# Four start-up edits to a fused attention and MLP kernel: where a tile of x and a weight piece are sent from, how the map weights are folded, and the order that goes with it

## The chip, the cores and the metric

The kernel runs on one core of one Trainium2 chip. The metric is device time in microseconds (us) from launch to end. The time before is 149.91 us, the median of five runs (149.40 to 150.06).

The engines: TensorE multiplies matrices (PE in the profile; PEld is its weight load), VectorE (DVE) and ScalarE (ACT) work on elements and read PSUM, GpSimd (POOL) does elementwise work on SBUF, SyncE (SP) issues transfers. ScalarE issues some too.

## The reference, cut to what matters

One sequence of 2048 tokens, width D = 448, sixteen heads of 28, an MLP of width 1792, all in bfloat16. Two branches read the same layernorm and are added to the input:

```python
xn  = layernorm(x)
qkv = xn @ wqkv                                   # q, k, v: 16 heads of 28
pq, pk = q @ w_phi[h], k @ w_phi[h]               # a 28x28 map for each head
phi = lambda p: concat([softmax(p), softmax(-p)]) # 56 features a head
kv  = sum_s phi(pk)[s]^T v[s];  z = sum_s phi(pk)[s]
o   = (phi(pq) @ kv) / (phi(pq) @ z + 1e-6)       # linear attention
out = x + o @ wo + silu(xn @ w1) @ w2
```

Since the map has no non-linearity ahead of it, the kernel multiplies each head's columns of wqkv by its map once (the fold), and then uses the folded weights `Wqk` directly on xn. A softmax does not change when the same number is taken from all its inputs, so the fold also takes each head's last column from the other 27, and that last feature's exponential is the constant one.

## The kernel before, in words

Tokens are in 16 tiles of 128. The head of the program loads x tile by tile and the first pieces of w1, takes the layernorm of tiles 0 to 3 (`ln_tile`: statistics `bnst`, `bnag`, the root `ve` on ScalarE for tiles 0 to 3 and on GpSimd after, `rstd`, the normalised tile `xn`), transposes these four tiles on TensorE (`tr0a` to `tr3`) and starts three MLP blocks on them. Tiles 4 to 15 are transposed by DMA from SyncE (`xnT_dma5`, `xnT_dma7` and so on, two tiles each).

After that the work is in blocks: `F` is a pair of 128-column pieces of the first MLP product for 512 tokens (F0 to F6 for tiles 0 to 3, F7 to F13 for 4 to 7, and so on), `v`, `k`, `q` are the projections of two tiles. Each block fills two PSUM banks. It runs as two halves (`a` with three pairs, `b` with four pairs of matmuls): each matmul takes 64 rows, the lower and the upper row half of the array work beside each other and write different banks, and in the second half of a block they change banks. ScalarE then reads the two banks (silu for F, exponentials for k and q, a copy for v). `f` is the fold, `K` the sums over keys, `M` their masking, `s` the scaling of query features by GpSimd followed by a DMA transpose into `phT`, `U` attention of one tile, `Y` and `F n@bank` the second MLP product of a tile, `W` and `R` the output projection, `E` the last tile.

TensorE's order is written out by hand in `PLAN`, one word for each step with its banks behind the `@`; `strict` makes every TensorE instruction keep that order. The other engines' orders come from a list scheduler (`_Prog.schedule`) with assumed durations; within an engine the emitted order is then fixed, and each instruction waits on semaphores for what it depends on. `chain` adds order between instructions of one engine.

SyncE issues nearly all loads, in order: x tiles 0, 1, 2 and 3, pieces of w1, x tiles 4 to 7, the rest of w1, wv, x tiles 8 to 11, three weight transposes (`wT_dma0` to 2, straight from wqkv in DRAM), x tiles 12 to 15, `xnT_dma5`, `xnT_dma7`, five more weight transposes, the other `xnT` transposes, w2 and wo. ScalarE issues the head maps (`wphi`) and the second w1 piece (`w1_512`, columns 512 to 1023, first used by the third MLP block of the head).

The fold (`fold`, `fold_loads`, `fold_mms`, `fold_sub`): GpSimd spreads the maps into block-diagonal matrices of four heads (`BDphi`, 112 rows, with `maskh`); eight transposes bring wqkv's columns in groups of 112; each fold step does two of the four row tiles (`kt`) of D with sixteen full-array matmuls, 112 rows by 112 columns; ScalarE copies each head's last column, VectorE subtracts it, one subtraction for each row tile.

Of the kernel before, what the change touches and what calls it, by code (L numbers as in the profile page):

```python
# [6 lines left out]
BF16 = mybir.dt.bfloat16  # L7
F32 = mybir.dt.float32
# [132 lines left out]
class _Prog:  # L141
# [76 lines left out]
    def schedule(self):  # L218
# [55 lines left out]
        while done < n:  # L274
# [58 lines left out]
          ("pool", "pe"): 100.0}  # L333
PLAN = """aF3@4 bF3 aF6@0 aF4@2 bF4 bF6 av2@4 aF5@6 bv2 bF5 av0@2 aF12@0 aF13@4 bv0 bF12 bF13 aF11@6 bF11 f2@24 aF8@0 aF10@6 bF8
bF10 f0@24 aF9@0 aF7@6 bF9 bF7 ak2@4 bk2 av12@6 ak14@2 bv12 av10@0 bk14 bv10 ak4@4 av14@6 bk4 ak0@2 bv14 ak8@0 bk0 bk8
av6@6 Y2@5:1 Y2:9 Y2:4 ak6@2 av8@0 bv6 bv8 bk6 av4@6 ak10@4 bv4 bk10 ak12@2 aq4@0 bk12 K0-2 bq4 aq6@4 K2-4 bq6 aq8@2
K4-6 bq8 aq0@0 aF17@4 s4 K6-10 bq0 aF14@2 bF17 bF14 aF19@0 K10-12 bF19 aF16@4 K12-16 aF23@2 bF16 bF23 aF27@0 aF24@4 bF27
bF24 M aF20@2 aF25@0 bF20 aF15@4 bF25 aF26@2 aF22@6 bF26 aF18@0 s6 s8 bF22 bF15 bF18 aq2@6 aF21@2 aq10@4 bF21 bq2 aq12@0
bq10 bq12 F7@3:8 Y0@6:7 U9 Y1@5:6 F6@4:14 Y1:3 s0 F9@2:11 U6@1 Y1:5 U5 U7@0 Y0:7 F9:3 s2 Y3@1:10 Y3:4 W9 s10 s12 U10
U3@5 W6 F7:6 aq14@0 R9,6 bq14 U8 W7 F5@4:8 s14 F10@5:7 U0 F10:7 U11@6 U12@1 F5:6 U4@2 F4@0:10 W5 F8@7:12 W10 F4:4 F8:2  # L340
U2@1 W4 W0@6 W3@2 W8 R4,3 R8 R0,7,10,5 F13@1:14 F11@2:3 F12@6:4 F14@5:7 W2@3 U1@4 U13 F14:7 F11:2 F11:3 F12:1 F11:4 U14
F11:1 F11:1 W11 W1@4 F12:9 W12 U15 W13 W14 R14,12 R13,11 R1,2 F15@07:5 F15:5 F15:4 E15"""


def bass_parallel_sum__linear_kernel_hedgehog__dense_activation_silu__prompt_kernel(
# [12 lines left out]
    KP = 112  # L358
    G = 4
# [16 lines left out]
    with es:  # L376
        def sb(name, shape, dt):
            return es.enter_context(nc.sbuf_tensor(name, shape, dt))
# [12 lines left out]
        DQ = H * DF  # L391
        Wqk = sb("Wqk", [128, 2, 4, DQ], BF16)
        last27 = sb("last27", [128, 4, 2, H], F32)
        Wp = sb("Wp", [KP, G, DH], BF16)
        BDphi = sb("BDphi", [KP, G, KP], BF16)

# [23 lines left out]
        ones_bf = sb("ones_bf", [128, 128], BF16)  # L420
        ones4 = sb("ones4", [KP, 4], F32)
        mtmp = sb("mtmp", [KP, 4], F32)
        maskh = sb("maskh", [KP, 4], F32)
        mask2 = sb("mask2", [KP, 2], F32)
# [37 lines left out]
        def d_pool(n, per=1.0):  # L462
            return n * per + 120.0
# [24 lines left out]
        def act(dst, src, func, n, name, scale=1.0, table=None, **keys):  # L488
            P.op("act", d_act(n), lambda e: e.activation(dst, src, func, scale=scale),  # L489
                 reads=[src], writes=[dst], table=table, name=name, **keys)  # L490
# [8 lines left out]
        def load(dst, src, name, eng="sp", lat=1700.0):  # L499
            n = 2  # L500
            for _, cnt in list(dst.ap):
                n *= cnt
            P.dma(lambda e: e.dma_start(out=dst, in_=src), n / 280.0, writes=[dst], name=name, eng=eng, lat=lat)  # L503

        load(Wp[:], A_w_phi.rearrange("(g hl) d f -> (hl d) g f", g=G), "wphi", eng="act", lat=2500.0)
        memset(ones_bf[:], 1.0, 128, "ones")
# [5 lines left out]
        memset(ones4[:], 1.0, 4, "ones4")  # L512
        act(warm_act[:], ones_bf[:, 0:4], ACTF.Sqrt, 1750, "warm_act", table="sqrt")

        def block_mask(dst, w, n):
            tmp = mtmp[:, 0:n]
            P.op("pool", d_pool(4), lambda e: e.affine_select(tmp, ones4[:, 0:n], [[-w, n]], ALU.is_ge, 0.0,
                                                               base=0, channel_multiplier=1),
                 reads=[ones4[:]], writes=[tmp], name="mask1")
            P.op("pool", d_pool(4), lambda e: e.affine_select(dst, tmp, [[w, n]], ALU.is_ge, 0.0,  # L520
                                                               base=w - 1, channel_multiplier=-1),
                 reads=[tmp], writes=[dst], name="mask2")

        block_mask(maskh[:], DH, 4)

# [6 lines left out]

        def load_x(t0, t1):
            load(x_sb[:, t0:t1, :], xt[:, t0:t1, :], f"x{t0}", lat=1400.0)

# [7 lines left out]
        load_x(0, 1)  # L543
        load_x(1, 2)
        load_x(2, 4)
# [6 lines left out]
        load_x(8, 12)  # L552
        load_x(12, 16)
        load(w2_sb[:], B_w2.rearrange("(f p) d -> p f d", p=128), "w2")
        for i in range(2):
# [9 lines left out]

        bd4 = BDphi[:].rearrange("p g (h f) -> p g h f", h=4)

        def fold():
            P.op("pool", d_pool(448, 2.0), lambda e: e.tensor_tensor(
                bd4, Wp[:, :, None, :].broadcast_to([KP, G, 4, DH]),  # L570
                maskh[:, None, :, None].broadcast_to([KP, G, 4, DH]), ALU.mult),
                reads=[Wp[:], maskh[:]], writes=[BDphi[:]], name="bdphi")

        def fold_loads():
            for a in range(8):
                dma_t(wT_sb[:, a, :], A_wqkv[:, a * KP:a * KP + 128], 600.0, f"wT_dma{a}", 1800.0 if a == 2 else 1310.0, sbuf=False)

        def fold_mms(k0, slots):
            mms = []
            for kt, fb in zip((k0, k0 + 1), slots):  # L580
                for qk in range(2):
                    wps = banks[fb + qk][:, 0:G * KP].rearrange("p (g c) -> p g c", g=G)
                    mms += [(wps[:, g, :], wT_sb[0:KP, qk * 4 + g, KS[kt]:KS[kt] + 128], BDphi[:, g, :], True, True) for g in range(G)]
            P.cur_slack = 400.0
            pe_mms(mms, "fold", dur=50.0 * len(mms))
            P.cur_slack = 0.0
            for kt, fb in zip((k0, k0 + 1), slots):
                src = psum[:, fb * 512:(fb + 2) * 512].rearrange("p (b c) -> p b c", b=2)[:, :, 0:D].rearrange("p b (h f) -> p b h f", f=DH)
                ref = last27[:, kt, :, :]
                act(ref, src[:, :, :, DF], ACTF.Identity, 32, "fold_ref")  # L590
                dst = Wqk[:, :, kt, :].rearrange("p b (h f) -> p b h f", f=DF)
                fold_sub(dst, src[:, :, :, 0:DF], ref)

        def fold_sub(dst, src, ref):
            P.op("dve", d_dve(2 * DQ), lambda e: e.tensor_tensor(dst, src, ref[:, :, :, None].broadcast_to([128, 2, H, DF]), ALU.subtract),
                 reads=[src, ref], writes=[dst], name="fold_sub")
# [119 lines left out]
        def proj_block(t, b0, is_k):  # L716
            fns = pair_block(b0, DQ, lambda i, kt, r: xnT[r, t + i, kt, :],
                             lambda i, kt, r: Wqk[r, int(is_k), kt, :], "k" if is_k else "q")

            def evac():  # L720
                E2 = ek(t, 2)[:, :, 0:2 * D] if is_k else eq(t, 2)
                src = psum[:, b0 * 512:(b0 + 2) * 512].rearrange("p (i c) -> p i c", i=2)[:, :, 0:DQ].rearrange("p i (h f) -> p i h f", f=DF)
                dst = E2.rearrange("p i (h s f) -> p i h s f", s=2, f=DH)
                for sg in range(2):
                    act(dst[:, :, :, sg, 0:DF], src, ACTF.Exp, 2 * DQ, "exp", scale=(1.0 if sg == 0 else -1.0), table="exp", okeys_w=["acttab"])
                E4 = E2.rearrange("p i (h f) -> p i h f", f=DH)
                R2 = Rec[:, int(is_k), t:t + 2, :]
                step = 2 if is_k else 1
                for i in range(0, 2, step):
                    sums(E4[:, i:i + step], R2[:, i:i + step, :], step)  # L730
                if is_k:
                    scale_rows(t, is_k)

            return *fns, evac
# [158 lines left out]
        chain("bnst0 bnag0 bnst1 bnag1 rstd0 xn0a xn0 rstd1 xn1 bnst2 bnag2 bnst3 bnag3 rstd2 xn2 rstd3 xn3 ev3".split())  # L893
        chain("wphi warm_act w1_512 ve0 ve1 ev0a ev0 ev1 ve2 ve3 ev2 silu_table".split())
        fold_loads()
# [24 lines left out]
        chain("ev3 bnst4".split())  # L920
        block_mask(mask2[:], 2 * DH, 2)
        memset(vaug[:, :, :, DH], 1.0, 2150, "vaug1")
# [6 lines left out]
        for t in range(8, NT):  # L929
            ln_tile(t)  # L930
        chain("x8 wT_dma0 wT_dma1 wT_dma2 x12 xnT_dma5 xnT_dma7 wT_dma3 wT_dma4 wT_dma5 wT_dma6 wT_dma7 xnT_dma9 xnT_dma11 xnT_dma13 xnT_dma15 w2 "
              "wo0 wor0 wo1 wor1".split())
# [18 lines left out]
        for word in PLAN.split():  # L951
# [10 lines left out]
            elif kind == "f":  # L962
                k0, slots = arg.split("@")
                fold_mms(int(k0), tuple(map(int, slots)))
            elif kind == "K":
# [141 lines left out]
```

The softmax here doesn't subtract the row's maximum and nothing guards it: scores larger than these inputs give would overflow.

## Time and profile before

| what | value |
|---|---|
| median of five runs | 149.91 us |
| the profiled execution, its own time | 149.91 us |
| its span | 148.6 us |
| TensorE busy | 144.2 us, 97% of the span, 1540 matmuls |
| VectorE, ScalarE, GpSimd busy | 90.2, 71.0, 71.3 us |
| matmul groups by line and form: MLP second product, 128x448 | 210, 42.4 us |
| MLP first product, 64x512 | 356, 41.1 us |
| k and q projections, 64x432 | 224, 23.7 us |
| fold, 112x112 | 32, 1.9 us |
| fold's subtractions on VectorE, 128x864 | 4, 4.0 us |
| x tile 0 issued, landed, first statistics | 0.80, 3.06, 3.09 us |
| first w1 piece on ScalarE's queue issued, landed | 1.31, 5.15 us |
| last DMA transpose of a weight group issued, landed | 23.50, 26.53 us |

The 1.3 us between time and span lie outside the profiled instructions. Busy times of matmuls contain their pipelined ends, so neighbouring matmuls overlap, and rates are read from the starts of neighbouring groups. A line of the timeline has its start, its busy time, engine, source line, operation, what is written and read, the number of instructions, and in brackets the idle time before it with what ended it.

### The profile page before, as it was taken

The page shows a single profiled execution, that of the slowest core. Times are in us where ns is not written, and L with a number is a line of the kernel's source. Part 1 is how long each engine was busy: PE and PEld are TensorE (multiplying, and loading weights), DVE is VectorE, ACT ScalarE, POOL GpSimd, SP SyncE. Part 2 cuts the span into 40 slices and gives each one's busy share as a digit, 9 for nine tenths or more (in the row PEclk, how much of TensorE's full clock was granted, in tenths as well). Part 3 has the DMA queues.
Part 4 walks back from the last instruction along what each step waited for, and adds up shares of the span by engine and source line. Part 5 has one row for each costly group of instructions (what it writes and reads, how often), then busy time and mean ns, then how long its engine had stood idle before and what let it go on. Part 6 is the DMA issues. An engine that isn't in the chain of part 4 may idle for free.

```text
span 148.6 us, 3656 instructions
## 1 busy us (share of the span) xinstructions
PE 144.2 (97%) x1540; PEld 79.6 (54%) x1540; DVE 90.2 (61%) x189; ACT 71.0 (48%) x88; POOL 71.3 (48%) x82
## 2 busy tenths in 40 slices
PE   7899999899999999999999999999999999999994
PEld 7694443454554456656444444555545655455563
DVE  1978996441399949504996003999477902815284
ACT  4568757357999399969655859400022000000000
POOL 7107566410069999998799900799000900000000
PEclk9999999999999999999999999999999999999999
DMA  4999953999700000000089570058789348732325
GB/s 103 373 381 188 302 106 65 191 179 358 206 3 4 0 0 7 0 4 4 0 154 167 106 141 4 0 101 172 150 83 195 72 74 168 154 108 48 62 67 184
DMA packets 44352, 17.42 MB, mean 117 GB/s; under 512 B 36912, under 2 KB 43952, under 8 KB 44336
## 3 DMA queue, kind: packets, MB, share of 16 engines
q1 hardware_dynamic: 41168, 14.99, 47.7%
q10 hardware_dynamic: 3168, 2.20, 4.8%
q8 instruction: 12, 0.20, 0.6%
q14 instruction: 4, 0.03, 0.1%
HBM read 6.56 MB, written 1.84 MB: 56 GB/s over the span
## 4 chain that ended last, share of the span: by engine, by line
PE 83%; DVE 11%; POOL 2%; DMA 2%; issue 1%; SPq 0%; DVEq 0%
PE psum L469 82%; DVE st L602 5%; DVE RA L617 4%; DMA x_sb<-in_A_x_dram 2%; DVE mv L603 1%; POOL Ek_sb L496 1%; POOL rstd L613 1%; PE psum L484 1%; DVE x_sb L855 1%; POOL ve L611 0%; DVE xnT L493 0%; SPq L503 0%; DVE rstd L608 0%; DVEq L1065 0%
## 5 line engine op out<-in xcount | busy, mean ns | idle before, releaser
L469 PE MATMUL psum<-xnT,phT 64*128 64x512 bf16 (+1 forms) x428 | 45.7, 350 | 0.3
L469 PE MATMUL psum<-w_sb,hT 128*128 128x448 bf16 (+1 forms) x238 | 45.2, 342 | 0.0
L737 DVE TENSOR_REDUCE Rec<-Ek_sb 128x32 f32<-128x896 bf16 (+1 forms) x20 | 24.3, 1247 | 27.2 <-ACT Ek_sb L489 19.6
L773 POOL TENSOR_TENSOR RA<-Ek_sb,Rec 128x896 bf16<-128x896 bf16 x16 | 27.0, 1721 | 21.5 <-DVE Rec L738 20.1
L489 ACT ACTIVATE hT<-psum 128x1024 bf16<-128x1024 f32 x28 | 27.2, 1023 | 13.2 <-PE psum L469 13.2
L469 PEld LDWEIGHTS psum<-w_sb,hT 128*128 128x128 bf16 x238 | 22.3, 98 | 18.7 <-issue 1.5
L469 PEld LDWEIGHTS psum<-xnT,phT 64*128 64x128 bf16 (+1 forms) x428 | 20.8, 95 | 21.1 <-PE psum L469 1.7
L489 ACT ACTIVATE Ek_sb<-psum 128x864 bf16<-128x864 f32 x24 | 20.3, 933 | 17.6 <-DVE x_sb L855 16.1
L469 PE MATMUL psum<-Wqk,xnT 64*128 64x432 bf16 x224 | 23.7, 343 | 0.1
L747 POOL TENSOR_TENSOR Ek_sb<-Ek_sb,Rec 128x896 bf16<-128x896 bf16 x8 | 13.4, 1699 | 9.1 <-ACT phT L489 9.1
L469 PEld LDWEIGHTS psum<-Wqk,xnT 64*128 64x128 bf16 x224 | 10.4, 95 | 10.1 <-PE psum L469 0.8
L747 POOL TENSOR_TENSOR phT<-phT,Rec 128x896 bf16<-128x896 bf16 x8 | 13.4, 1699 | 0.0
L469 PE MATMUL psum<-wv,xnT 64*128 64x448 bf16 x112 | 12.7, 349 | 0.0
L602 DVE BATCH_NORM_STATS2 st<-x_sb 128x6 f32<-128x448 bf16 x16 | 9.7, 604 | 3.2 <-DMA x_sb<-in_A_x_dram 3.1
L469 PE MATMUL psum<-wo_sb,vaug 128*128 128x448 bf16 (+1 forms) x51 | 11.0, 341 | 0.0
L833 DVE TENSOR_SCALAR den<-psum 128x16 f32<-128x16 f32 x16 | 2.3, 155 | 13.2 <-PE psum L469 13.2
L840 DVE TENSOR_TENSOR vaug<-psum,rden 128x448 bf16<-128x448 f32 x16 | 9.8, 623 | 0.4
L489 ACT ACTIVATE vaug<-psum 128x896 bf16<-128x896 f32 x8 | 7.4, 936 | 5.1 <-PE psum L469 5.0
L617 DVE TENSOR_SCALAR RA<-x_sb,mv,rstd 128x384 bf16<-128x384 bf16 (+4 forms) x29 | 8.9, 346 | 1.4 <-POOL rstd L613 1.2
L855 DVE TENSOR_TENSOR x_sb<-psum,x_sb 128x448 bf16<-128x448 f32 (+1 forms) x13 | 7.1, 583 | 2.9 <-PE psum L469 2.9
L738 DVE RECIPROCAL Rec<-Rec 128x32 f32<-128x32 f32 (+1 forms) x24 | 8.6, 391 | 0.1
L469 PEld LDWEIGHTS psum<-wv,xnT 64*128 64x128 bf16 x112 | 5.5, 94 | 5.2
(51 smaller groups left out, 106.9 us busy)
## 6 DMA issues: line engine op xcount, KB each, us to landing
out_dram<-x_sb ACTq DMA_DIRECT2D x15, 112.0 KB, 1.8
w_sb<-in_B_w_dram SPq DMA_DIRECT2D x1, 1568.0 KB, 8.8
x_sb<-in_A_x_dram SPq DMA_DIRECT2D x3, 448.0 KB, 6.3
wo_sb<-in_A_wo_dram SPq DMA_DIRECT2D x2, 336.0 KB, 8.5
phT<-in_B_w_dram SPq DMA_DIRECT2D x1, 576.0 KB, 6.4
phT<-in_B_w_dram SPq DMA_DIRECT2D x2, 256.0 KB, 4.5
phT<-in_B_w_dram ACTq DMA_DIRECT2D x1, 384.0 KB, 3.8
wv<-in_A_wqkv_dram SPq DMA_DIRECT2D x1, 336.0 KB, 6.8
```

Source lines behind the costliest of these rows:

```text
L469: r = e.matmul(dst, lhsT, rhs, start=st, stop=sp, skip_group_check=True)
L484: r = e.transpose(dst, src, ident[:])
L489: P.op("act", d_act(n), lambda e: e.activation(dst, src, func, scale=scale), reads=[src], writes=[dst], table=table, name=name, **keys)
L602: P.op("dve", 590, lambda e: e.bn_stats(st6[:, t, :], xs), reads=[xs], writes=[st6[:, t, :]], name=f"bnst{t}", okeys_w=["ln"])
L617: P.op("dve", dur, lambda e: e.tensor_scalar(dst, x_sb[:, t, c0:c1], mv[:, t, 0:1], rstd[:, t:t + 1], ALU.subtract, ALU.mult), reads=[xs, ...
L737: P.op("dve", 50 + 967 * n, lambda e: e.tensor_reduce(R2, E4, AXL.X, ALU.add), reads=[E4], writes=[R2], name="Ssum")
L738: P.op("dve", 135 + 210 * n, lambda e: e.reciprocal(R2, R2), reads=[R2], writes=[R2], name="Rrec")
L747: P.op("pool", 1700, lambda e: e.tensor_tensor(E3, E3, Rk[:, :, None].broadcast_to([128, 32, DH]), ALU.mult), reads=[E3, Rk], writes=[E3], ...
L773: P.op("pool", 1700, lambda e: e.tensor_tensor(dst, Eq, Rq.rearrange("p (c j) -> p c j", c=CC)[:, :, :, None].broadcast_to([128, CC, 4, DH ...
L833: P.op("dve", 190, lambda e: e.tensor_scalar(den[:, uq, :], U3[:, :, DH], EPS_DEN, None, ALU.add), reads=[U3[:, :, DH]], writes=[den[:, uq ...
L840: P.op("dve", 620, lambda e: e.tensor_tensor(o3, U3[:, :, 0:DH], rden[:, uq, :, None].broadcast_to([128, H, DH]), ALU.mult), reads=[U3[:, ...
L855: P.op("dve", d_dve(cs.stop - cs.start), lambda e: e.tensor_tensor(res[:, cs], ob, addend[:, cs], ALU.add), reads=[ob, addend[:, cs]], wri ...
```

## The change

- Tile 1 of x is issued by ScalarE, first in its queue, where `wphi` stood; SyncE issues tile 0 and then tiles 2 and 3.
- `w1_512`, issued by ScalarE, now waits on the semaphore of the first activation (`warm_act`), where it only followed it in order.
- The head maps are loaded by four SyncE transfers after x tiles 12 to 15 and ahead of `xnT_dma5`, into two tiles that GpSimd first sets to zero.
- The fold takes 64-row matmuls of two heads (56 columns) that alternate between the lower and upper row half and between two banks: sixteen for each of the four row tiles, so four steps `f` in place of two. There are nine weight transposes in place of eight, six of them after `xnT_dma7`. Each step is followed by two column copies on ScalarE and three subtractions on VectorE. The layout of `Wqk` follows.
- `PLAN` is a new order of the same blocks: the first fold step comes after F3, F4, F6, v2, F5, v0, F12, F11, F13 and the first halves of F10 and F8; the other three come between the following halves.

```diff
-PLAN = """aF3@4 bF3 aF6@0 aF4@2 bF4 bF6 av2@4 aF5@6 bv2 bF5 av0@2 aF12@0 aF13@4 bv0 bF12 bF13 aF11@6 bF11 f2@24 aF8@0 aF10@6 bF8
-bF10 f0@24 aF9@0 aF7@6 bF9 bF7 ak2@4 bk2 av12@6 ak14@2 bv12 av10@0 bk14 bv10 ak4@4 av14@6 bk4 ak0@2 bv14 ak8@0 bk0 bk8
...
-F11:1 F11:1 W11 W1@4 F12:9 W12 U15 W13 W14 R14,12 R13,11 R1,2 F15@07:5 F15:5 F15:4 E15"""
+PLAN = """aF3@4 bF3 aF4@0 aF6@2 av2@6 bF4 bF6 aF5@4 av0@0 bv0 bF5 aF12@2 bv2 aF11@0 aF13@4 bF12 bF11 bF13 aF10@6 aF8@0 f0@2 f3@4
+bF8 bF10 f2@2 aF9@0 f1@4 aF7@6 bF9 bF7 ak2@4 bk2 av12@6 av10@0 ak14@2 bv12 bk14 bv10 ak4@4 av14@6 bk4 ak0@2 bv14 av6@0
...
+U2 W4 U6@3 U3@5 W7 W9 s12 W0@2 R4,7 aq14@3 R0,9 bq14 Y3@5:2 Y3:3 U5@2 U1 F5@6:5 F5:9 U8@2 F6@0:11 F6:3 Y3:5 U13@2 U11
+F11@4:14 Y3:2 U10@3 s14 W2@2 W5 W6 U12 F14@3:6 F10@1:7 U14 Y3:2 F10:7 F14:6 W10 F13@7:10 F14:2 W11 W14 R6,14 R5,10 R2,11
+F13:4 F8@5:8 F8:4 F8:2 W3@6 W8 W13 F12@1:2 F12:1 F12:11 U15@0 W12 W1@4 R1,8,13 R12,3 F15@23:6 F15:8 E15"""
...
-        load(Wp[:], A_w_phi.rearrange("(g hl) d f -> (hl d) g f", g=G), "wphi", eng="act", lat=2500.0)
...
-        load_x(1, 2)
+        load_x(1, 2, "act")
...
+        phi = A_w_phi.rearrange("h d f -> (h d) f")
+        P2 = 2 * DH
+        load(Wp[8:8 + KP, 0:3, :], phi[P2:P2 + 3 * KP, :].rearrange("(g p) f -> p g f", g=3), "wphi")
+        load(Wp[8:64, 3, :], phi[D - P2:D, :], "wphi1")
+        load(Wp[64:64 + P2, 3, :], phi[0:P2, :], "wphi2")
+        load(Wp0[0:P2, :], phi[0:P2, :], "wphi3")
...
         def fold_loads():
-            for a in range(8):
-                dma_t(wT_sb[:, a, :], A_wqkv[:, a * KP:a * KP + 128], 600.0, f"wT_dma{a}", 1800.0 if a == 2 else 1310.0, sbuf=False)
+            for i in range(NW):
+                c = max(0, KP * i - 64)
+                dma_t(wT(i), A_wqkv[:, c:c + 128], 600.0, f"wT_dma{i}", 1800.0 if i == 2 else 1310.0, sbuf=False)
...
+        def fold_mms(kt, b):
+            PW = 2 * DH
+            lo, hi = slice(0, 64), slice(64, 128)
             mms = []
+            for i in range(NW):
+                w = wT(i)[:, KS[kt]:KS[kt] + 128]
+                mms.append((banks[b][:, PW * i:PW * i + PW], w[lo], BD[lo, (i - 1) % G, :] if i else BD0[:], i == 0, i == NW - 1))
+                if 0 < i < NW - 1:
+                    mms.append((banks[b + 1][:, PW * (i - 1):PW * i], w[hi], BD[hi, (i - 1) % G, :], i == 1, i == NW - 2))
             P.cur_slack = 400.0
-            pe_mms(mms, "fold", dur=50.0 * len(mms))
+            pe_mms(mms, "fold", dur=26.0 * NW, mode=64, tiles=(b, b + 1))
             P.cur_slack = 0.0
...
-        chain("wphi warm_act w1_512 ve0 ve1 ev0a ev0 ev1 ve2 ve3 ev2 silu_table".split())
+        chain("x1 warm_act w1_512 ve0 ve1 ev0a ev0 ev1 ve2 ve3 ev2 silu_table".split())
+        byname = {o.name: o for o in P.ops}
+        byname["w1_512"].deps.add(byname["warm_act"].id)
+        byname["w1_512"].odeps -= byname["w1_512"].deps
...
-        chain("x8 wT_dma0 wT_dma1 wT_dma2 x12 xnT_dma5 xnT_dma7 wT_dma3 wT_dma4 wT_dma5 wT_dma6 wT_dma7 xnT_dma9 xnT_dma11 xnT_dma13 xnT_dma15 w2 "
+        chain("x8 wT_dma0 wT_dma1 wT_dma2 x12 wphi wphi1 wphi2 wphi3 xnT_dma5 xnT_dma7 wT_dma3 wT_dma4 wT_dma5 wT_dma6 wT_dma7 wT_dma8 xnT_dma9 xnT_dma11 xnT_dma13 xnT_dma15 w2 "
               "wo0 wor0 wo1 wor1".split())
```

## The prediction

> **What bounds the kernel now.** I read the page's busy times and slices first, then TensorE's timeline, then SyncE's and VectorE's for whoever ends its waits.
>
> ```profile
> PE 144.2 (97%) x1540; PEld 79.6 (54%) x1540; DVE 90.2 (61%) x189; ACT 71.0 (48%) x88; POOL 71.3 (48%) x82
> ...
> PE   7899999899999999999999999999999999999994
> ...
> DMA  4999953999700000000089570058789348732325
> ```
>
> TensorE is busy 97% of the span and its row has one weak place after the head: the 8 in the eighth slice, 26.0 to 29.7 us. The matmuls run one behind another to 146.3 us, and then come 0.77 us of VectorE and the last store. So whatever time TensorE loses or saves passes to the end one for one, unless a later wait takes it. TensorE's timeline (start, busy time, instruction):
>
> ```profile
> 22.49 3.64 PE L469 MATMUL psum<-xnT,phT 64*128 64x512 bf16 x30
> 26.66 0.95 PE L469 MATMUL psum<-BDphi,Y_sb 112*128 112x112 bf16 x16 [0.53 <-POOL Ek_sb L496]
> 27.54 3.20 PE L469 MATMUL psum<-xnT,phT 64*128 64x512 bf16 x28
> 30.67 0.96 PE L469 MATMUL psum<-BDphi,Y_sb 112*128 112x112 bf16 x16
> 31.56 3.19 PE L469 MATMUL psum<-xnT,phT 64*128 64x512 bf16 x28
> 34.59 1.68 PE L469 MATMUL psum<-Wqk,xnT 64*128 64x432 bf16 x14
> ...
> 56.41 0.66 PE L469 MATMUL psum<-vaug,Ek_sb 64*128 64x58 bf16 x32
> 56.91 1.44 PE L469 MATMUL psum<-Wqk,xnT 64*128 64x432 bf16 x14
> ```
>
> Start-to-start times are what counts. From 31.56 to 34.59 fourteen pairs of 64-row matmuls take 3.03 us, 0.216 a pair. From 27.54 to 30.67 the same fourteen take 3.13, because a full-array fold follows: a change between 64 and 128 rows costs 0.10. The folds take 0.88 and 0.89 us with the change back. The line at 22.49 has one pair more than the next but is 0.44 longer, not 0.22: its block's second half follows its own first half directly (`aF11@6 bF11`), and the row halves swap banks; that costs 0.22. Its matmuls are issued out by 25.96, with the change 26.06, and the fold starts at 26.66: a wait of 0.60. The GpSimd memset named there has nothing to do with the fold. The DMA queue shows the real releaser (SyncE's timeline, then the landing of the DMA issued at 23.5):
>
> ```profile
> 13.52 3.77 SPq L560 DMA_TRANSPOSE xnT<-RA  x2
> 17.33 7.44 SPq L560 DMA_TRANSPOSE Y_sb<-in_A_wqkv_dram  x5
> 24.81 5.45 SPq L560 DMA_TRANSPOSE xnT<-RA  x4
> ```
>
> ```profile
> L560 SPq DMA_TRANSPOSE Y_sb<-in_A_wqkv_dram x1: 1262/1262/1262, 23.5 to 23.5; - x1
> DMA to landing us min/median/max: 3.0/3.0/3.0
> ```
>
> The eighth weight transpose (`wT_dma7`) is issued at 23.50 and lands at 26.53. It comes after `xnT_dma7` on SyncE, which waits for layernorm of tile 7. That is the second chain.
>
> **Fold matmuls and mode changes.** Before: 0.88 + 0.89 + two changes into it, 1.97 us. After: 64 matmuls with 64 rows, 128 columns and 56 moving columns. The nearest row is the 64x58 one: 32 in 0.50 us (56.41 to 56.91), so 64 cost 1.00, and no mode changes. Saving 0.97. The other end of the price is the old fold's 49 ns a matmul, 3.1 us, a loss of 1.2; I take the 64x58 row, which has this shape.
>
> The Trainium skill speaks against this: TensorE: Matmul & The Clock Gate, Back-to-back issue gap, gives small matmuls a floor of about 25 ns from start to start. With it the folds would take an estimated 1.6 us and the forecast would be about 149.8; the trace shows 15.6 ns for row pairs, and the trace decides.
>
> **Second half after its own first half.** The old plan has it four times (F3, F4, F11, k2), the new three (F3, v0, k2): -0.22.
>
> **The head.** Tile 1 of x landed at 4.05 (issued 1.26, 2.8 us), and VectorE, done with tile 0's statistics at 3.93, waited for it:
>
> ```profile
> 1.26 2.79 DMA x_sb<-in_A_x_dram
> 4.05 0.03 issue
> 4.08 0.64 DVE st L602
> ```
>
> That is the chain of waits. Issued at 0.80 on ScalarE's queue and with `w1_512` held back, tile 1 lands at 3.1 to 3.6, before 3.93, so the layernorm chain gains 0.13; tile 0 now shares the engines with it, so it may lose up to 0.15 or gain as much where the 56-byte rows of the head-map weights (`wphi`) are gone. I take a gain of 0.10. The held-back `w1_512` goes out after the first activation ends at 2.74; behind it on ScalarE waits `ve0`, at 4.03, and one issue takes 0.45: no delay. Its first user is the third head block, at 8.4; it lands at 6.6 by its own old 3.84 us, and by the slowest weight row (6.4) at 9.2, 0.8 late, which the wait before the fold would cover.
>
> **Late map weights.** Four issues of 0.42 to 0.58, 1.7 to 2.3 us, go into SyncE's pause from 11.75 to 13.52, which the missing tile-1 issue lengthens by 0.46: at most 0.1 late. GpSimd's products (0.93 us before, fewer elements now) and new masks lie in its pauses; if it waits for the weights' landing near 18 us, layernorm of tiles 10 to 13 slips by up to 0.5, hidden because their transposes now queue behind one more weight transpose.
>
> **The ninth weight transpose.** Six instead of five after `xnT_dma7`: the last goes where an `xnT` transpose went, at 24.81, and lands 3.03 later, 27.84, or 27.75 with the head's gain; TensorE starts 0.1 after. Its own readiness: 25.96, less 0.22, plus the first halves of F10 and F8, which the plan puts ahead (six pairs, 1.30): 27.03. So it waits 0.82 against 0.60: +0.22. The head's gain is lost in this wait. Bounds: no wait at all (-0.60) to a transpose issue that blocks as one did (2.24 against 1.26): +1.2. The later `xnT` transposes slip 1.26 to land by 33.5 (v12 starts near 35), w2 to 40.4 (Y2 near 44.6): covered.
>
> **Evacuating four folds.** VectorE's row:
>
> ```profile
> 27.95 2.02 DVE L595 TENSOR_TENSOR Wqk<-psum,last 128x864 bf16<-128x864 f32 x2 [2.53 <-ACT last L489]
> ```
>
> Four subtractions become twelve of 54, 432 and 378 elements. From 448 elements in 0.62 and 224 in 0.39 they take 0.22, 0.60 and 0.54, overlapping by 0.08: 1.12 a fold. From the start of fold 0, TensorE reaches `ak2` after 1.00 of folds and 22 pairs, 5.75 us. VectorE starts at 0.75 (0.25 fold, 0.5 to the first subtraction as at 27.95), ends folds 0 and 3 at 2.99; fold 2's column copies stand behind two silus of 0.92 on ScalarE, to 3.7; folds 2 and 1 are done at 5.95, the signal at 6.05. `ak2` needs all four: +0.30. Bounds: 0, and 0.9 if one more silu is ahead.
>
> **Sum.** -0.97 - 0.22 + 0.22 + 0.30 = -0.67. All other blocks are the same in number and row packing; every other mode change stays. The profiled execution took 149.91, the median too, span 148.6; so 149.2, span about 147.9. Later waits: the last `K` group moves with GpSimd's chain (ended 68.67, group at 69.15), which starts from `ak2` and moves with it.
>
> **The rivals.** *The transposes keep up*: the ninth lands by 26.9, because queue blocking (one issue of 2.24 between five) was the old delay. Then 0.82 of wait and 0.1 of head are gained too: 148.3. Against it: the extra issue is certain.
>
> *The transposes eat it*: a second blocked issue adds 0.98 to the landing, part of it is already likely: 149.9 to 150.2. For it: of SyncE's transpose issues from 9.4 to 24.8, four took over 1.5.
>
> *Slower: the late query transpose.* The new order asks for tile 14's attention (`U14`) near 124.5; the old at 136.7. What it needs came late:
>
> ```profile
> 115.25 3.35 POOL L773 TENSOR_TENSOR RA<-Ek_sb,Rec 128x896 bf16<-128x896 bf16 x2 [11.37 <-DVE Rec L738]
> ```
>
> ```profile
> 110.23 12.46 SPq L560 DMA_TRANSPOSE vaug<-vaug  x7
> 122.79 1.34 SPq L560 DMA_TRANSPOSE phT<-RA  x1
> ```
>
> GpSimd was done at 118.6, but the transpose stood behind seven others till 122.79 and landed at 128.0, 19.4 after `aq14` began. `aq14` moves to near 106.9: 126.3, a wait of 1.8 before `U14`, so 151.0. It decides once the landing is later than 124.5; without the 4.2 us in the queue it lands at 122.1 and costs nothing.
>
> **How the numbers follow.** Forecast as summed 0.45 (own range 148.9 to 149.6); transposes keep up 0.20; transposes eat it 0.20; late query transpose 0.15. A change under 0.3%, 0.45 us, is about what measuring this kernel can't tell from none. Faster by more: four fifths of the first and all of the second, 0.56. Slower: the last and a little of the third, 0.18. Within: 0.26. The range runs from the second case to the upper end of the third, 148.2 to 150.4, and leaves out the last.
>
> **What would show it.** Fold 0 near 27.8, its wait after the ninth landing, 64 fold matmuls at under 16 ns, no 0.10 steps around them, `ak2` near 33.9 with a short wait for VectorE, tile 1's statistics following tile 0's without a gap. Wrong: fold 0 by 27.0 or past 28.5, a wait at `U14`, or fold matmuls of 25 ns and more.

## Result and profile after

The changed kernel takes 151.12 us (median of 43 runs, 149.77 to 153.28), the kernel before 149.78 in the same sitting. The ratio is 1.0074, 95% interval 1.0058 to 1.0090: slower by 0.7%, where 149.2 was forecast with a range of 148.2 to 150.4. The ratios here leave disturbed runs out, and the kernel before took 149.84, 149.86 and 150.26 in the three sittings of the experiments, so kernels of different sittings are compared by their ratios.

The profiled execution took 151.21 us with a span of 150.0, 1.30 us more than before. Its busy times and slices:

```profile
PE 143.8 (96%) x1572; PEld 79.6 (53%) x1572; DVE 91.5 (61%) x197; ACT 71.8 (48%) x92; POOL 71.5 (48%) x88
...
PE   7689999899999999999999999999899999999994
...
DMA  4999974697950000000188391076799576305024
```

TensorE has less work than before and a longer span. Its row has three weak places: a 6 and an 8 in the second and third slices (3.7 to 11.2 us), the old 8 ahead of the fold (26.2 to 30.0), and a new 8 at 105.0 to 108.7. TensorE's timeline at these places:

```profile
5.76 1.05 PE L491 MATMUL psum<-ident,RA 128*128 128x128 bf16 x8 [0.46 <-DVE RA L652]
7.75 1.05 PE L476 MATMUL psum<-xnT,phT 128*128 128x128 bf16 x16 [0.94 <-ACT ve L641]
9.10 0.62 PE L476 MATMUL psum<-xnT,phT 128*128 128x128 bf16 x8 [0.30 <-DMA phT<-in_B_w_dram]
...
29.14 0.39 PE L476 MATMUL psum<-BD,Y_sb 64*128 64x56 bf16 x16 [0.54 <-DMA wT<-in_A_wqkv_dram]
...
35.22 0.72 PE L476 MATMUL psum<-Wqk,xnT 64*128 64x432 bf16 x6
...
105.45 0.74 PE L476 MATMUL psum<-wo_sb,vaug 128*128 128x448 bf16 x3 [0.19 <-DMA vaug<-vaug]
106.02 0.62 PE L476 MATMUL psum<-KVm,phT 112*128 112x58 bf16 x16
106.48 0.73 PE L476 MATMUL psum<-wo_sb,vaug 128*128 128x448 bf16 x3
107.45 1.31 PE L476 MATMUL psum<-wo_sb,vaug 128*128 128x448 bf16 x6 [0.23 <-DMA vaug<-vaug]
```

In the head, tile 0 of x lands at 3.58, 0.52 later than before, and TensorE stands from 6.8 to 7.75 and from 8.8 to 9.10 for rows of w1 (`w1_0` landed at 7.61, `w1_0r` at 9.05; before, 6.51 and 7.25). The 64-row stage starts at 12.78 instead of 11.37, the first fold at 29.14 instead of 26.66, released by the weight transpose. From there to the first key projection it takes 6.08 us. The two output-projection lines late in the order (W4 at 105.45, W9 at 107.45) wait for the transposes of the attention output; from the starts, with the matmuls' own time taken off, these waits are 0.35 and 0.40 us.

SyncE's timeline shows what the transpose queued behind, and the query on the transposes of that stretch when it landed:

```profile
12.72 0.58 SPq L510 DMA_DIRECT2D x_sb<-in_A_x_dram  x1
13.35 3.05 SPq L510 DMA_DIRECT2D Wp<-in_A_w_phi_dram  x4
16.45 2.67 SPq L577 DMA_TRANSPOSE xnT<-RA  x2
19.16 6.83 SPq L577 DMA_TRANSPOSE Y_sb<-in_A_wqkv_dram  x5
26.02 1.26 SPq L577 DMA_TRANSPOSE wT<-in_A_wqkv_dram  x1
```

```profile
L577 SPq DMA_TRANSPOSE wT<-in_A_wqkv_dram x1: 1256/1256/1256, 26.0 to 26.0; - x1
...
DMA to landing us min/median/max: 3.0/3.0/3.0
```

The ninth transpose is issued at 26.02 and lands at 29.01, where 27.75 was forecast. Its own issue (1.26) and landing time (2.99) are those expected; it stands later in the queue. The chain of waits now begins with weights instead of tile 1 of x:

```profile
2.22 6.83 DMA phT<-in_B_w_dram
9.05 0.05 issue
9.10 0.62 PE psum L476 x8
```

The last view is a table of stretches, once for the kernel before and once for the changed one. In each row stand the stretch and its length, then busy time (instructions) of TensorE, weight load, VectorE, ScalarE and GpSimd, then the clock, the DMA engines' share and their GB/s.

```profile
3.50:5.00 1.50, 1.50 (x17) 1.50 (x15) 1.25 (x5) 0.34 (x2) 0.79 (x1) 1.00 1.06 374
5.00:7.00 2.00, 1.48 (x18) 0.88 (x17) 1.92 (x7) 1.32 (x4) 0.00 (x0) 1.00 1.12 366
```

```profile
3.50:5.00 1.50, 1.50 (x17) 1.50 (x15) 1.32 (x4) 0.29 (x1) 0.36 (x2) 1.00 0.72 168
5.00:7.00 2.00, 1.25 (x11) 0.56 (x9) 1.89 (x8) 1.11 (x4) 0.00 (x0) 1.00 1.05 327
```

Between 3.5 and 5.0 us the changed kernel moves 168 GB/s instead of 374: 0.31 MB less in 1.5 us. From 5 to 12 us both kernels run the DMA engines at 327 to 393 GB/s, so nothing is caught up, and 0.31 MB at 380 GB/s is an estimated 0.8 us. The engines' share falls by less than their rate, from 1.06 to 0.72: part of the missing bytes is idle time and part is slower transfers, and no run here shows why.

### The profile page after: what moved, and what is told of

Same layout as the page of the kernel before. It is cut to its first block, busy times and chain, and to the rows that moved or that the text cites. A ratio compares the mean times of both kernels' runs of the same rounds, so it can differ in the third digit from the quotient of the medians.

```text
span 150.0 us, 3741 instructions
## 1 busy us (share of the span) xinstructions
PE 143.8 (96%) x1572; PEld 79.6 (53%) x1572; DVE 91.5 (61%) x197; ACT 71.8 (48%) x92; POOL 71.5 (48%) x88
## 4 chain that ended last, share of the span: by engine, by line
PE 78%; DMA 8%; SPq 5%; DVE 5%; issue 1%; POOL 1%
PE psum L476 78%; DMA phT<-in_B_w_dram 5%; SPq L577 4%; DVE st L637 2%; DMA wT<-in_A_wqkv_dram 2%; DMA vaug<-vaug 2%; DVE RA L652 1%; SPq L510 1%; DVE mv L638 1%; DVE x_sb L890 1%; POOL rstd L648 0%; PE psum L491 0%; DVE xnT L500 0%; POOL ve L646 0%
## 5 line engine op out<-in xcount | busy, mean ns | idle before, releaser
L476 PE MATMUL psum<-xnT,phT 64*128 64x512 bf16 (+1 forms) x428 | 45.1, 350 | 1.3 <-ACT ve L641 0.9
L476 PEld LDWEIGHTS psum<-xnT,phT 64*128 64x128 bf16 (+1 forms) x428 | 21.3, 95 | 21.2 <-ACT ve L641 1.1
```

What stands on the lines that cost most here:

```text
L476: r = e.matmul(dst, lhsT, rhs, start=st, stop=sp, skip_group_check=True)
```

## The experiments

**Theory.** The hold on `w1_512` makes the DMA engines move fewer bytes in the first microseconds; all loads, and behind them SyncE's queue and the ninth weight transpose, come later by that much, and the fold waits for it. The late output projections are a second, separate cost. **Rivals:** the new place of tile 1, the fold itself with its twelve subtractions, or the order.

**1. No hold** (changed kernel, tile 1 still on ScalarE's queue).

```diff
-        byname["w1_512"].deps.add(byname["warm_act"].id)
```

> The changed kernel, with the second w1 piece no longer waiting for the first activation; all else equal, every engine's order too. Theory H (the hold leaves the transfer engines half idle from 3.5 to 5 us, so the first two w1 pieces land at 7.6 and 9.05 instead of 6.5 and 7.25 and the head ends 1.4 us late): second w1 piece lands near 5.2 again, the first two near 6.6 and 7.4, the 64-row stage starts near 11.4 instead of 12.8, and the time falls by 1.1 to 1.4, to 149.7 to 150.0. Theory Q (tile 1 on ScalarE's queue next to tile 0 is what slows the start: tile 0 landed 3.58 instead of 3.06): little change, 150.7 to 151.1. Theory L (the loss is later, in the waits before the output projections at 105 to 107): no change in time, whatever the head does.

149.85 us, ratio 1.0013 [0.9976, 1.0051], below the changed kernel's interval: nearly all of the loss is gone. Its stretch and its first fold:

```profile
3.50:5.00 1.50, 1.42 (x17) 1.25 (x15) 1.32 (x3) 0.29 (x1) 0.36 (x2) 1.00 1.04 370
```

```profile
28.17 0.39 PE L476 MATMUL psum<-BD,Y_sb 64*128 64x56 bf16 x16 [0.42 <-DMA wT<-in_A_wqkv_dram]
```

The rate is back at 370 GB/s, the 64-row stage starts at 11.63, the ninth transpose lands 0.97 earlier (28.04), and the fold starts as much earlier. The two late waits stay (0.37 and 0.29).

**2. Tile 1 back on SyncE, hold kept.**

```diff
-        load_x(1, 2, "act")
+        load_x(1, 2)
```

> The changed kernel with tile 1 of x back on SyncE's queue behind tile 0; the second w1 piece still waits for the first activation. Theory H: the w1 pieces are as late as in the changed kernel (7.6 and 9.05, each up to 0.5 later), the time stays at 150.9 to 151.4. Theory Q: tile 0 lands near 3.06 again, the head gains 0.5 to 1.4, the time is 149.7 to 150.6. Theory L: 151.1.

150.38 us, 1.0041 [1.0007, 1.0075]: between the two, within the range of the rival (tile 1's place slows the start) and below that of the theory. Tile 0 landed at 2.93; it lands at 2.91 to 3.06 in the profiles with tile 1 on SyncE and at 3.20 to 3.59 in those with tile 1 on ScalarE. With nothing ahead of it on ScalarE the piece was issued at 2.33 instead of 2.76, and the stretch had 326 GB/s; the ninth transpose landed at 28.33. So this run made the hold shorter as well, and says little of tile 1's place by itself. The first run says more: there tile 1 stays on ScalarE, and the loss is gone.

**3. Both edits of the head undone.**

> The changed kernel with both edits of the head taken back (tile 1 on SyncE, no wait of the second w1 piece): what is left of the change is the fold, the late map weights and the order. Theory H: as the run without the hold, 149.6 to 150.0. Theory Q: as the run with tile 1 on SyncE. If hold and queue each cost a part: the lowest of the three, 149.3 to 149.6. By the terms of my sum (fold -0.97, second half -0.22, transposes +0.22, evacuation +0.30) and the 0.75 of waits before the output projections: the kernel before and +0.1, 149.9. Theory L: 151.0.

150.36 us, 1.0057 [1.0018, 1.0097], above the 149.6 to 150.0 of the theory; the interval overlaps that of the changed kernel and that of the first run, so this run doesn't say which of the two it is like. With the map weights gone from ScalarE's queue the second w1 piece goes out at 1.04, ahead of tile 1 on SyncE (1.27), and tile 1 landed at 4.68. In this profiled execution TensorE was also at half speed until 9.9 us (last section), so its head can't be compared with the others. Behind the fold three output projections wait, 0.87 us in all (the account below).

**4. Late output projections moved back** (W4, W7, W9 behind four steps of Y3 and U3).

```diff
-U2 W4 U6@3 U3@5 W7 W9 s12 W0@2 R4,7 aq14@3 R0,9 bq14 Y3@5:2 Y3:3 U5@2 U1 F5@6:5 F5:9
+U2 U6@3 U3@4 Y3@5:4 W4 W7 W9 s12 W0@2 R4,7 aq14@3 R0,9 bq14 Y3:1 F5@6:3 U5@2 U1 F5:2 F5:9
```

> The changed kernel with the output projections of tiles 4, 7 and 9 moved behind four matmuls of the second MLP product of tile 3, which were to follow later, and the banks and pieces of tiles 3 and 5 moved with it. Theory L (SyncE's transposes for tiles 4 and 9 land at 105.4 and 107.4, after the projections are due, and that wait of 0.35 and 0.40 passes to the end): the two waits go, the time falls by 0.6 to 0.75, to 150.3 to 150.5. Theory H alone (something later takes these 0.75 again, so that only the head counts): 150.9 to 151.1.

151.85 us, 1.0115 [1.0069, 1.0160]: no better than the changed kernel, where 150.3 to 150.5 was expected. The waits near 105 and 107 went, and another came at U14, 1.16 us by the starts:

```profile
126.76 0.39 PE L476 MATMUL psum<-KVm,phT 112*128 112x58 bf16 x8 [0.99 <-DMA phT<-RA]
```

The last query transpose was issued at 122.31 and landed at 126.63, 1.73 later than in the changed kernel (124.90, where U14 did not wait). That is the late query transpose of the prediction's third rival: its mechanism exists, but in the changed kernel it lands 1.60 us before U14 starts (126.50).

**5. The hold alone, on the kernel before.**

```diff
+        byname = {o.name: o for o in P.ops}
+        byname["w1_512"].deps.add(byname["warm_act"].id)
+        byname["w1_512"].odeps -= byname["w1_512"].deps
```

> The kernel before, with one edit: the second w1 piece waits for the first activation. My theory (holding the piece back leaves the DMA engines half idle in the first microseconds, and every later weight row lands later): w1_512 is issued near 2.7 instead of 1.3, the two w1 pieces on SyncE's queue land no earlier than before (6.5 and 7.2 us) and the 64-row stage starts 0.8 to 1.4 us later than 11.4, the end moves by 0.6 to 1.4: 150.5 to 151.2 us. Rival (the hold costs only beside tile 1 on ScalarE's queue, which takes the engines from SyncE's pieces): within 0.3 us of the kernel before, 149.5 to 150.1 us.

151.31 us, 1.0068 [1.0031, 1.0106]: the one edit costs as much as the whole change. The profiled execution (150.04) was among the quickest of this kernel, so its trace understates it; even there the stretch has 298 GB/s, the 64-row stage starts at 12.14, and the two first pieces landed at 6.07 and 8.17. But its first fold starts at 26.92, only 0.26 later than before: where the other executions lose 1 us this trace doesn't show.

**6. The fold alone** (third run with the order of before, `f2@24` as `f2@2 f3@4`, `f0@24` as `f0@2 f1@4`).

> The changed kernel with both edits of the head undone and the order of the kernel before (the four folds put where its two stood): only the fold in 64-row passes and its late map weights are left. Theory (the fold itself saves about 0.9 us of TensorE, but the ninth weight transpose and the map weights' four issues on SyncE's queue make the fold wait; the rest of the new order costs the waits ahead of the output projections): the fold waits 1.0 to 1.5 us for the ninth transpose, TensorE does not wait ahead of the output projections, and the total is 149.0 to 149.7 us. Rival (the fold in 64-row passes loses by itself, through twelve subtractions instead of four): a wait of over 0.6 us ahead of the first key projection, 150.0 to 150.6 us.

152.26 us, 1.0159 [1.0107, 1.0211]. The wait ahead of the first fold was 0.95, there was no wait ahead of the first key projection, and none ahead of the first output projections; but another came, 0.86 ahead of an output projection at 139.61, and the total was far above both expectations. Neither expected that the order of before would not suit the new fold. What the fold alone is worth in time, this run therefore doesn't say.

**7. No hold, and three words of the order exchanged.** W7, whose transpose lands first, goes ahead of U6; W4 after U3; W0 ahead of W9.

```diff
-U2 W4 U6@3 U3@5 W7 W9 s12 W0@2 R4,7 aq14@3 R0,9
+U2 W7 U6@3 U3@5 W4 s12 W0@2 W9 R4,7 aq14@3 R0,9
```

> The changed kernel without the hold (as in the first experiment, profiled at 150.14) and with three words of the order exchanged: W7 ahead of U6, W4 after U3, W0 ahead of W9. Theory (the two waits near 104.1 and 105.9 us, 0.37 and 0.29, come from the landing of the attention transposes of tiles 4 and 9, which follow each other by 1.26 us or more on SyncE's queue): both waits go, no new one over 0.15 appears at U14, and the end moves by 0.5 to 0.7 us: 149.0 to 149.4 us. Rival (a later wait takes what is gained, at U14 or at the last tile): 149.7 to 150.0 us, with a new wait of 0.3 us or more after 120 us.

148.99 us, 0.9962 [0.9931, 0.9993]: faster than the kernel before and than the changed one. The same stretch as above, from its TensorE timeline:

```profile
103.82 0.73 PE L476 MATMUL psum<-wo_sb,vaug 128*128 128x448 bf16 x3
104.38 0.62 PE L476 MATMUL psum<-KVm,phT 112*128 112x58 bf16 x16
104.84 1.93 PE L476 MATMUL psum<-wo_sb,vaug 128*128 128x448 bf16 x9
```

No wait is left, and none over 0.15 us comes after the fold's own two. The order now asks for the transposes in the order in which SyncE issues them.

**8. The seventh run, with the map weights loaded after the fifth weight transpose.**

```diff
-x12 wphi wphi1 wphi2 wphi3 xnT_dma5 xnT_dma7 wT_dma3 wT_dma4 wT_dma5
+x12 xnT_dma5 xnT_dma7 wT_dma3 wT_dma4 wphi wphi1 wphi2 wphi3 wT_dma5
```

> As the run before it, and the four map-weight loads go out after the fifth weight transpose instead of ahead of the transposes of tiles 4 to 7. Theory (ahead of them the four issues take 3.7 us of SyncE's queue, 2.4 of them one blocked issue, and push the ninth weight transpose): the four issues take under 2.2 us in all, the ninth transpose lands 0.4 to 1.2 us earlier than 28.0, the wait ahead of the first fold (0.5) shrinks to 0.1 or less, and the total is 0.3 to 0.5 us under the run before it: 148.6 to 149.0 us. Rival (the queue is full wherever they stand, or the fold then waits for the map products of GpSimd): the fold starts no earlier than 28.0 and the total is that of the run before it, within 0.2 us.

150.82 us, 1.0068 [1.0027, 1.0110]: the theory fell. SyncE's timeline:

```profile
10.92 0.58 SPq L510 DMA_DIRECT2D x_sb<-in_A_x_dram  x1
13.51 3.61 SPq L577 DMA_TRANSPOSE xnT<-RA  x2
17.16 2.56 SPq L577 DMA_TRANSPOSE Y_sb<-in_A_wqkv_dram  x2
19.76 3.29 SPq L510 DMA_DIRECT2D Wp<-in_A_w_phi_dram  x4
```

The four issues take 3.29 us here (1.78 to 3.68 in the place that the change gives them), and the pause from 11.5 to 13.5, in which SyncE waits for layernorm, is empty again. The ninth transpose lands at 29.46 instead of 27.73, 1.73 later, and the median is 1.83 later. Of these two places for the map weights, the one that the change gives them is the cheaper.

**9. The sixth run with tile 1 on ScalarE's queue.**

> The changed kernel without the hold and with the order of the kernel before: against the sixth run, only tile 1 of x goes out on ScalarE's queue. Theory (with the map weights gone from ScalarE's queue, the second w1 piece goes out at 1.04 there, ahead of tile 1 on SyncE's, and tile 1 lands a microsecond late, 4.7 to 5.1 against 4.05; that cost the third and sixth run their head): tile 1 lands by 3.6, the 64-row stage starts at 11.3 to 11.8 and the total falls by 0.5 to 1.5 us under the 152.26 of the sixth run, to 150.8 to 151.7; the wait ahead of the first fold (0.95 there) stays or grows to 1.5, since SyncE's queue sets it. Rival (the old order and the new fold do not fit each other, and the head has no part in it): 152.0 to 152.5 us.

152.77 us, 1.0159 [1.0095, 1.0223]: the ratio of the sixth run again, as the rival has it (the median lies 0.3 above its range). Tile 1 landed at 3.60 and the 64-row stage started at 11.71, and TensorE only waits longer:

```profile
27.89 0.39 PE L476 MATMUL psum<-BD,Y_sb 64*128 64x56 bf16 x16 [1.41 <-DMA wT<-in_A_wqkv_dram]
...
139.38 0.74 PE L476 MATMUL psum<-wo_sb,vaug 128*128 128x448 bf16 x3 [0.60 <-DMA vaug<-vaug]
...
147.61 0.46 PE L476 MATMUL psum<-wo_sb,vaug 128*128 128x224 bf16 x3 [0.38 <-DMA vaug<-vaug]
```

**10. The third run, with the head's loads as before:** a load of the maps into a tile that nobody reads stands ahead of the w1 piece.

> The third experiment (both edits of the head undone), and on ScalarE's queue, ahead of the second w1 piece, a load of the map weights into a tile that nobody reads, as the kernel before has it: the head's loads are those of the kernel before in order and time. Theory (the third experiment was slow, 150.36, because the second w1 piece moved ahead of tile 1): the piece is issued at 1.3, tile 1 lands at 3.5 to 4.1 and the total is 149.6 to 150.0 us, as without the hold (149.85). Rival (the third experiment's head was slow by the clock granted late, 9.9 us, and not by tile 1): tile 1 lands at 4.5 or later again, or the total stays at 150.2 to 150.5.

150.36 us, 1.0025 [0.9984, 1.0066]. Tile 1 landed at 4.44 and the piece was issued at 1.31; the interval overlaps those of the first and the third run. In its trace the first fold starts at 27.89, as early as in any run of the new order but one, and three output projections wait behind it, 1.00 us in all. Whether tile 1 behind the piece was that run's loss stays open.

**11. The seventh run, with the second w1 piece on SyncE, behind the first two.** Nothing is held.

```diff
-        load_w1(512, 1024, "act")
+        load_w1(512, 1024)
```

> The seventh run (no hold, output order mended, 148.99 us) with the second w1 piece on SyncE's queue behind the first two pieces instead of alone on ScalarE's. Theory (the DMA engines are fed from two queues in the first 5 us, and what they leave idle there is lost): the first pieces land no earlier, the second at 8.5 us or later, the 64-row stage starts at 12.3 or later, and the total is 0.5 to 1.3 us above the run it changes: 149.5 to 150.3. Rival (the held-back piece only takes the engines from the first two pieces at the wrong moment): the first two land earlier (by 6.0 and 7.0), the second by 8.4, the stage starts by 11.9 and the total is 148.8 to 149.3.

150.46 us, 1.0025 [0.9991, 1.0058]. The stretch, and TensorE at the first fold and the last tile:

```profile
3.50:5.00 1.50, 1.50 (x17) 1.36 (x15) 1.39 (x6) 0.36 (x2) 0.36 (x2) 1.00 0.77 180
```

```profile
28.79 0.39 PE L476 MATMUL psum<-BD,Y_sb 64*128 64x56 bf16 x16 [1.12 <-DMA wT<-in_A_wqkv_dram]
...
146.80 0.46 PE L476 MATMUL psum<-wo_sb,vaug 128*128 128x224 bf16 x3 [0.67 <-DMA vaug<-vaug]
```

This run parts two things that the hold had mixed. The pieces landed at 5.97, 6.71 and 7.82, and the 64-row stage started at 11.35, as early as in any run: the rival's numbers. But the rate is 180 GB/s, near the changed kernel's 168, the ninth transpose lands at 28.65, and the time is lost: the theory's total. A late head on TensorE is therefore not needed for the loss: the fold starts 0.93 later than in the seventh run, by SyncE's queue. The rest of what this trace loses is mostly the wait of 0.84 at the last tile. The edit also adds an issue of 0.47 us to that queue, half of the 0.92 by which the ninth transpose moved, so this 0.92 is shared between the rate and the issue, and this run doesn't say how. The Trainium skill, DMA: Bandwidth & Descriptors, Issuing engines are not separate DMA queues, says that starting transfers from several engines saves only issue time, since the sixteen DMA engines are shared. In this stretch the measurement differs: between 3.5 and 5.0 us the rate was 322 to 381 GB/s in the eight profiles whose second piece went out on ScalarE's queue at 1.0 to 1.3 us, 168 to 326 in the five with the hold, and 180 here.

**12. The changed kernel, hold and all, with the order of the seventh run.**

> The changed kernel, hold and all, with only the three words of the order exchanged (W7 ahead of U6, W4 after U3, W0 ahead of W9). Theory (the waits of 0.35 and 0.40 us near 105 and 107 us are a cost of its own, independent of the head's): both go and the time falls by 0.6 to 0.9 us under the changed kernel's 151.07: 150.2 to 150.5 us. Rival (with the late head something else is later there, and the waits come back elsewhere): 150.8 to 151.2 us.

150.52 us, 1.0024 [0.9991, 1.0057], against 1.0074: half a per cent, 0.75 us, as much as the two waits of the changed kernel. Its trace has no wait over 0.16 us after the fold starts. So the order's cost stands by itself. Here the first fold doesn't wait for the transpose (no bracket), because TensorE itself is late, with the 64-row stage at 13.56:

```profile
29.23 0.39 PE L476 MATMUL psum<-BD,Y_sb 64*128 64x56 bf16 x16
```

Against the seventh run only the hold differs: 1.0024 against 0.9962. With the changed kernel against the first run (1.0074, 1.0013) and the fifth against the kernel before (1.0068) that makes three pairs that differ by the hold alone, and each time it costs 0.6 to 0.7%, 0.9 to 1.0 us.

**The account.** In the traces of the new order without a clock drop the end follows from two things, the start of the first fold and the waits of output projections and attention behind it (us; the kernel before, in its own order, for comparison):

| kernel | ninth (before: eighth) transpose landed | first fold | last matmul starts | end less fold | waits late in the order | rest |
|---|---|---|---|---|---|---|
| before | 26.53 | 26.66 | 146.30 | 119.64 | 0.12 | 119.52 |
| changed | 29.01 | 29.14 | 147.58 | 118.44 | 0.35 + 0.40 | 117.69 |
| 1, no hold | 28.04 | 28.17 | 146.52 | 118.35 | 0.37 + 0.29 | 117.69 |
| 2, tile 1 on SyncE | 28.33 | 28.47 | 147.32 | 118.85 | 0.29 + 0.48 + 0.38 | 117.70 |
| 3, old head | 28.23 | 28.73 | 147.29 | 118.56 | 0.32 + 0.30 + 0.25 | 117.69 |
| 4, late projections | 28.88 | 29.02 | 147.84 | 118.82 | 1.16 | 117.66 |
| 7, no hold, order | 27.73 | 27.86 | 145.60 | 117.74 | 0.06 | 117.68 |
| 10, old head's loads | 27.75 | 27.89 | 146.60 | 118.71 | 0.37 + 0.29 + 0.34 | 117.71 |
| 11, piece on SyncE | 28.65 | 28.79 | 147.49 | 118.70 | 0.17 + 0.84 | 117.69 |
| 12, hold, order | 28.80 | 29.23 | 147.00 | 117.77 | 0.09 | 117.68 |

The last wait of the runs 2, 3, 10 and 11 is the one at the last tile. In them, and in the ninth run, which has it too, the last attention transpose took 2.98 to 3.55 us from issue to landing; in the nine profiles without this wait it took 2.51 to 2.60. No run here isolates why, so this part of these single traces may be chance.

## Why the prediction was wrong, step by step

- **Bound: right.** TensorE and SyncE's weight transposes were named as the two chains; the first fold starts 0.13 or 0.14 us after the last landing in every trace of the table but the third and the twelfth, where TensorE itself came later.
- **Fold: right.** From the fold's start to the last matmul the prediction has 145.63 less 27.85, 117.78; the traces have 117.66 to 117.71 with the later waits taken off. Two folds in a row, from 29.14 to 29.61, take 0.47 us: 14.7 ns a matmul, where 15.6 was taken and the floor of 25 ns (the Trainium skill, TensorE: Matmul & The Clock Gate, Back-to-back issue gap) would have given an estimated 0.8. In the last fold of the trace the two matmuls of a pair start 3 to 4 ns apart and the pairs 25 to 29 ns apart, so the floor could still hold for each row half; no run tests that. The changes of row mode around the folds are gone.
- **Second half after its own first half: right.** Three are left (at 13.87, 19.81 and 35.61), 0.22 each.
- **Evacuation: right.** VectorE ends the last subtraction 5.93 us after the first fold's start, 5.95 forecast, and `ak2` starts at 6.08, 6.05 forecast. Half of TensorE's wait falls one block earlier, at the first half of F9, which waits for ScalarE to empty its banks.
- **The ninth weight transpose: the number right, by errors that cancel.** Without the hold it lands at 27.73 and 28.04 (runs 7 and 1), forecast 27.75. But `xnT_dma5` was to start at 13.52 to 13.62 and starts at 15.52 and 15.77, behind the map weights; from there to the ninth issue it takes 9.62 and 9.72 us instead of 11.29; and that issue, at 25.14 and 25.49 instead of 24.72, lands after 2.59 and 2.55 us instead of 3.03.
- **The head: this is the step that failed.** It was priced at a gain of 0.10 us, from tile 1's landing (3.39, as forecast) and from the held piece's landing against its first user on TensorE, with the sentence that the wait before the fold would cover 0.8 of delay. The piece was followed to its reader, and not to the transfers around and behind it, and both sides of that wait moved. On TensorE the first two w1 pieces came late, the 64-row stage starts 1.41 later than before, and in the two traces in which the fold waits for nothing (runs 3 and 12) it starts 15.66 and 15.67 us after that stage. So TensorE would have been ready at an estimated 28.45, 0.60 past the forecast fold. On the other side the ninth transpose landed still later, at 29.01, 1.26 past the forecast, and that set the start of the fold. Taking the hold out moves this landing by 0.97 (run 1) and 1.07 (run 7 against 12). How the missing bytes reach it is shown only in part: of the 0.97, 0.53 is a later issue and 0.44 a longer time from issue to landing; of the 1.07, 0.69 and 0.38. In the fifth run SyncE is 1.41 late at x tiles 12 to 15 (12.58 against 11.17) and only 0.25 at the last weight transpose (23.75 against 23.50): its queue took up most of the delay. Tile 0, which was to lose up to 0.15, lost 0.52.
- **Late map weights: mis-sized.** Forecast 1.7 to 2.3 us of issues, measured 3.05, because single issues took longer, up to 2.4 in the first run. The eleven profiles with the loads in this place have 1.78 to 3.68, five of them under 2.2. The tile transposes behind them were to be at most 0.1 late and were 2.0 and 2.25 late in runs 7 and 1; the ninth transpose hides it (above).
- **Later waits: missed.** U14 was checked, the first output projections were not. W4 and W9 wait 0.75 us in all for transposes that SyncE issues 1.2 to 2.4 us apart between 100 and 108 us.
- **Sum.** 149.2 plus 1.29 (fold at 29.14 instead of 27.85) plus 0.75 is 151.24; the profiled execution took 151.21.
- **The rivals.** "The transposes eat it" came nearest, with the landing 1.26 later, by another cause than one blocked issue, and with too small a price. The late query transpose did not decide here, and did in the fourth run. In the seventh, without the other waits, U14 starts at 124.52 as forecast, and the transpose had landed at 122.80, not at 126.3.

## What to carry to other kernels

When a load is held back at a start that is bound by DMA, price the bytes that are then not moved, at the full rate, and carry them along every queue that issues behind them, as far as its pauses don't take them up; the reader of that one load can be the wrong place to look. When an order is written anew, take each step that reads a DMA transpose and set its place against the issue order and spacing of that queue, the first users as well as the late ones. A chain that ends in a wait has two sides, and a delay is covered by it only if the other side does not share the cause.

## What was not expected of the hardware

The granted clock fell during a wait. In the eighth run TensorE stood for 2.4 us ahead of the first fold; its slices of granted clock, and stretches from there:

```profile
PEclk9999999869999999999999999999999999999999
```

```profile
29.25:32.66 3.41, 3.06 (x44) 2.37 (x46) 2.16 (x6) 0.83 (x5) 0.00 (x0) 0.50 0.94 180
32.66:36.00 3.34, 3.33 (x59) 2.01 (x57) 1.47 (x6) 2.07 (x6) 0.00 (x0) 1.00 0.98 178
```

The drop begins at 29.25, 2.08 us after TensorE's last matmul ended (27.17) and 0.35 before the fold starts. For 3.41 us the clock was 0.50, and from the fold to the first key projection it took 7.48 us instead of 6.08. With waits of up to 1.4 us at the same place none of the other profiled executions shows a drop; whether the wait is its cause, one profile can't say. The Trainium skill, TensorE: Matmul & The Clock Gate, Part 1, gives a window of that length and says that its phase is free-running.

The head starts at half speed, and when that ends differs between executions: in the third run 24 matmuls of 128 columns took 2.58 us, 107 ns each, until 9.8 us, and the next twelve 56 ns each, which others reach between 4.5 and 7 us. The clock in the tables of stretches reads 1.00 there all the same, so the spacing has to be read.

```profile
7.18 2.79 PE L476 MATMUL psum<-xnT,phT 128*128 128x128 bf16 x24
9.76 0.48 PE L491 MATMUL psum<-ident,RA 128*128 128x128 bf16 x4
10.07 0.83 PE L476 MATMUL psum<-xnT,phT 128*128 128x128 bf16 x12
```

One profile of a kernel with such a head can mislead by a microsecond; the medians and the parts behind the fold are what the account above rests on.
